# Moving the switch from 8-tile to 16-tile chunks in an edge-sorting message-passing kernel

## The chip, the core and the metric

The kernel runs on one core of a Trainium2 chip. A core has five engines with a queue each: TensorE (PE; PEld is its weight loads), VectorE (DVE), ScalarE (ACT), GpSimd (POOL) and SyncE (SP). Indirect DMAs are issued from POOL, plain loads and stores from SP. The metric is the time of one execution on the device in microseconds (us); less is better. The kernel before was run three times, 11277.25, 11285.53 and 11288.28 us, median 11285.53.

## What is computed

One layer of message passing over a graph with 12,500 nodes of 64 features and 800,000 edges with 16 attributes; every edge has a source and a destination drawn at random.

```python
m_in = jnp.concatenate([x[src], x[dst], e_attr], axis=-1)
msg = _silu(m_in @ w_msg)
agg = _segment_sum(msg, dst, N)
return _silu(jnp.concatenate([x, agg], axis=-1) @ w_upd)
```

## The kernel before

The product with `w_msg` is split: node tables hold `x @ w_msg` for the source part (`A_d`, in memory) and for the destination part (`BW`, on chip). What is left for an edge is a row of `A_d` fetched by its source, a row of `BW` picked by its destination, and the attributes' product. To make the destination part local, the edges are first sorted into 128 buckets of 98 nodes, in memory (`st`), and then worked off in tiles of 128 edges of one bucket. Both halves run together, in one loop of *periods*.

**Sorting.** The edges lie in 6,250 tiles of 128. A *step* takes 8 tiles (`M`). It builds a one-hot of each edge's bucket (`onehot`, L397 and L398, ScalarE), running counts of the buckets over the tiles (`sums` or `halves`, L414 to L425, VectorE and ScalarE), ranks by matmul (`count`, L434 to L440, TensorE, then the reduce L445 on VectorE), spreads each edge's 17-number record to the slot of its rank (`expand`, L455 to L459, VectorE; tile `X`), and sums the tiles by matmul into a block `pl` with a row for each bucket (`move`, L476 and L478, TensorE). ScalarE copies the block (L483, L485) and POOL writes it to the buckets' ends in `st` by one indirect DMA, the *scatter* (L503). The pointers move on by the counts (`place`, L498 and L499).

A block gathers a *chunk*. The first `N8` chunks are one step long (8 tiles, turn 3 in the code), the later ones two steps (16 tiles, turns 0 and 1). `LIM[k]` is the number of slots that the first k+1 tiles of a chunk may fill in a bucket: 10 to 24 for the first eight, 27 to 36 for the second eight. A record has 17 numbers, so the second half's matmuls are 461 to 614 columns wide; what passes 512 goes to a second matmul (L478) into a free part of the PSUM bank of the batch's sums (`ag`). A chunk of 8 multiplies its tiles in falling order of width, a chunk of 16 in rising order.

**Groups and batches.** As soon as whole units of sorted tiles are known to lie in the store, a *group* of them is formed: a prefix sum over the buckets by matmul (L598), a list of tiles (L602 to L604), loads of the tiles from `st` (SP, L586). A group is cut into *batches*, one in a period: POOL gathers rows of `A_d` by source (`gather`, L666, one indirect DMA for each tile), VectorE builds one-hots of the destination (L676), TensorE transposes them (L685), multiplies by `BW` (L694) and, after the sum and the silu (L698, L699), sums the messages by destination (`reduce`, L715, into `ag`), and VectorE adds these sums to `ACC` (L727).

The groups grow. First come 64 tiles in batches of 8, then 640 tiles in groups of 24 with batches of 6 (two tiles to a unit), which are formed *quickly* (L598 right behind the ranks), then groups of 64 with batches of 8 (four tiles to a unit). When a group may be formed is decided while the program is built, by drawing sixteen random histories of the buckets (`Draws`) and waiting until all of them hold enough tiles. A chunk's tiles enter these histories when the chunk ends.

**The order in a period** is written out in `period`: each engine runs its part of the step and of the batches in this order, and each engine's queue keeps it.

```python
if q: q.gather(0, BT // 2)
if s: s.scatter()
if q: q.gather(BT // 2, BT)
```

So a scatter stands between the two halves of a batch's gathers. On TensorE a period holds the ranks of one step, the prefix sum if a quick group is formed, the transposes and sums of the batches, the placing matmuls of the step before, and the batch's product. On VectorE it holds the batch's one-hots, the group's lists, the rank reduce, the batch's sum and the adding to `ACC`, the running counts and the expansion.

After the last step (781) the loop goes on with batches alone until all sorted tiles are used (the *tail*), and the node update closes the kernel.

Of the kernel before, what the change touches and what calls it, by code (L numbers as in the profile page):

```python
# [21 lines left out]
MAGIC = 12582912.0  # L22
M = 8
C = 16
N8 = 140
LIM = [10, 13, 15, 17, 20, 21, 23, 24, 27, 28, 29, 30, 32, 34, 35, 36]
S = LIM[-1]
S8 = LIM[M - 1]
# [21 lines left out]
def mpnn_kernel(tc, x, e_attr, src, dst, w_msg, w_upd, out):  # L50
# [4 lines left out]
    assert E % P == 0 and NB <= NBK and NT >= C  # L55
    K8 = min(N8, NT // (2 * M))
    NCH = K8 + (NT - K8 * M + C - 1) // C
# [1143 lines left out]
```

## Time and profile before

| | |
|---|---|
| median of three runs | 11285.53 us |
| profiled execution | 11177.2 us |
| its span, first to last instruction | 11175.3 us |
| mean granted TensorE clock | 0.881 |
| gathers / scatters in it | 6322 / 460 grouped on one line, 461 in all |
| sort steps | 782 |

The profile is of one execution. It gives, for each engine, the time in which instructions ran; for groups of instructions of a line, their number, busy time and mean; for idle time, what ended it; and all of this for any window of the span. A row of the windows view is: the window, its length, then busy time and instructions of PE, PEld, DVE, ACT and POOL, the granted clock, the DMA share and GB/s. With a line chosen it has the busy time of that line's instructions alone. Matmuls in single precision appear as two records each.

### The profile page before, as it was taken

The page shows a single profiled execution, that of the slowest core. Times are in us where ns is not written, and L with a number is a line of the kernel's source. Part 1 is how long each engine was busy: PE and PEld are TensorE (multiplying, and loading weights), DVE is VectorE, ACT ScalarE, POOL GpSimd, SP SyncE. Part 2 cuts the span into 40 slices and gives each one's busy share as a digit, 9 for nine tenths or more (in the row PEclk, how much of TensorE's full clock was granted, in tenths as well). Part 3 has the DMA queues.
Part 4 walks back from the last instruction along what each step waited for, and adds up shares of the span by engine and source line. Part 5 has one row for each costly group of instructions (what it writes and reads, how often), then busy time and mean ns, then how long its engine had stood idle before and what let it go on. Part 6 is the DMA issues. An engine that isn't in the chain of part 4 may idle for free. (4 is left out here: it accounts for less than half of the span.)

```text
span 11175.3 us, 161538 instructions
## 1 busy us (share of the span) xinstructions
PE 9256.5 (83%) x51526; PEld 6296.5 (56%) x51526; DVE 7890.1 (71%) x17695; ACT 4917.0 (44%) x12471; POOL 6460.2 (58%) x6801
## 2 busy tenths in 40 slices
PE   7788888888888888888888888888888888888566
PEld 5566655555555555555555555555555555555455
DVE  7777777777677777777777777777777777777232
ACT  6455544444444444444444444444444444444111
POOL 2566655555555555555556555555555555555555
PEclk9999989989898988899999898899998988999655
DMA  3122211111111111211111111111111111111222
GB/s 96 44 51 50 51 45 42 44 40 44 39 43 40 44 39 41 45 41 42 42 41 44 42 40 43 40 40 42 43 41 43 41 43 40 43 42 39 41 39 45
DMA packets 667987, 490.31 MB, mean 44 GB/s; under 512 B 497911, under 2 KB 534967, under 8 KB 667127
## 3 DMA queue, kind: packets, MB, share of 16 engines
q0 software_dynamic: 237264, 338.54, 13.8%
q1 hardware_dynamic: 429543, 141.28, 6.0%
q8 instruction: 413, 6.77, 0.3%
q14 instruction: 447, 3.66, 0.1%
q10 hardware_dynamic: 320, 0.07, 0.0%
HBM read 330.05 MB, written 141.12 MB: 42 GB/s over the span
## 5 line engine op out<-in xcount | busy, mean ns | idle before, releaser
L666 POOL DMA_INDIRECT g<-A_d,sidx x6322 | 5993.1, 948 | 3438.0 <-issue 1686.2
L476 PE MATMUL pl<-X,hf 128*128 128x512 f32 (+10 forms) x12512 | 5005.5, 536 | 303.8 <-issue 255.1
L476 PEld LDWEIGHTS pl<-X,hf 128*128 128x128 f32 x12512 | 2358.1, 203 | 1669.7 <-issue 1145.5
L459 DVE TENSOR_TENSOR X<-cb,rec 128x442 f32<-128x442 f32 (+7 forms) x3128 | 2953.7, 1007 | 27.0
L397 ACT ACTIVATE hf<-iof,shi 128x128 f32<-128x128 f32 x6256 | 1908.5, 391 | 985.4 <-remote 569.6
L688 ACT ACTIVATE qt<-tq 114x1024 f32<-114x1024 f32 (+1 forms) x818 | 808.1, 988 | 2392.6 <-remote 1574.5
L727 DVE TENSOR_TENSOR ACC<-ag,ACC 64x98 f32 x1986 | 509.8, 257 | 1538.4 <-remote 1173.7
L445 DVE TENSOR_REDUCE rank<-z 128x8 f32<-128x1024 f32 x782 | 954.3, 1220 | 690.9 <-remote 387.1
L416 DVE TENSOR_TENSOR G<-G,hf 128x128 bf16<-128x128 bf16 x4173 | 1221.1, 293 | 144.9 <-ACT hf L398 4.0
L694 PEld LDWEIGHTS pre<-w,qt 114*128 114x128 f32 x10368 | 1243.2, 193 | 127.4 <-issue 117.8
L694 PE MATMUL pre<-w,qt 114*128 114x64 f32 x10368 | 1246.6, 274 | 24.9 <-issue 15.1
L478 PEld LDWEIGHTS ag<-X,hf 128*128 128x128 f32 x2568 | 549.4, 220 | 1161.5 <-issue 678.3
L483 ACT ACTIVATE blk<-pl 128x512 f32<-128x512 f32 (+1 forms) x461 | 263.2, 571 | 2133.1 <-PE pl L476 1674.8
L503 POOL DMA_INDIRECT st<-blk,ptrs x460 | 460.4, 1001 | 1183.2 <-ACT blk L485 910.8
L685 PE MATMUL tq<-ident,q 128*114 128x128 f32 x6322 | 981.7, 301 | 178.6 <-issue 125.4
L715 PE MATMUL ag<-q,g 128*64 128x98 f32 x12644 | 892.4, 276 | 278.1 <-issue 224.9
L685 PEld LDWEIGHTS tq<-ident,q 128*114 128x114 f32 x6322 | 844.5, 151 | 376.8 <-issue 191.2
L715 PEld LDWEIGHTS ag<-q,g 128*64 128x64 f32 x12644 | 683.7, 152 | 474.3 <-issue 405.0
L398 ACT ACTIVATE hf<-hf,ones 128x1024 f32<-128x1024 f32 x782 | 899.4, 1150 | 25.4
L676 DVE TENSOR_TENSOR q<-cb,lo 128x784 f32<-128x784 f32 (+1 forms) x818 | 768.6, 940 | 81.3 <-PE cb L598 32.3
L478 PE MATMUL ag<-X,hf 128*128 128x34 f32 (+3 forms) x2568 | 501.2, 280 | 360.2 <-DVE ACC L727 347.3
L434 PE MATMUL z<-hf,w 128*128 128x512 bf16 x1564 | 646.5, 413 | 7.8 <-ACT hf L398 5.0
(144 smaller groups left out, 5561.9 us busy)
## 6 DMA issues: line engine op xcount, KB each, us to landing
g<-A_d,sidx POOLq DMA_INDIRECT x6322
ea<-in_e_attr SPq DMA_DIRECT2D x260, 192.0 KB
rt<-st SPq DMA_DIRECT2D x1296, 34.0 KB
rt<-st SPq DMA_DIRECT2D x498, 8.5 KB
st<-blk,ptrs POOLq DMA_INDIRECT x460
nodes<-in_x SPq DMA_DIRECT2D x62, 98.0 KB
ACC<-rt SPq DMA_DIRECT2D x11, 544.0 KB
rt<-st SPq DMA_DIRECT2D x320, 17.0 KB
```

Source lines behind the costliest of these rows:

```text
L397: nc.scalar.activation(c.hf[:, k, :], iof, AF.Square, bias=c.hi[:, k:k + 1])
L398: nc.scalar.activation(c.hf, c.hf, AF.Relu, bias=ones, scale=-1.0)
L416: nc.vector.tensor_tensor(out=at(k), in0=c.hf[:, k - 2, :] if c.pos[k - 1] == 1 else at(k - 1), in1=c.hf[:, k - 1, :], op=OP.add)
L445: nc.vector.tensor_reduce(out=c.rank, in_=c.z, axis=AX.X, op=OP.max)
L459: nc.vector.tensor_tensor(out=c.x[:, k:k + 2, 2:2 + n * R].rearrange("p k (s c) -> p k s c", c=R), in0=hit[:, k:k + 2, 0:n, None].to_broad ...
L476: nc.tensor.matmul(pl[:, 0:min(w, 512)], c.hf[:, k, :], c.x[:, k, 0:min(w, 512)], start=n == first, stop=n == last, skip_group_check=True)
L478: nc.tensor.matmul(pl2[:, 0:w - 512], c.hf[:, k, :], c.x[:, k, 512:w], start=n == WIDE, stop=n == last, skip_group_check=True)
L666: j = nc.gpsimd.indirect_dma_start(out=t.g[:, i, :], out_offset=None, in_=A_d, in_offset=bass.IndirectOffsetOnAxis(ap=t.grp.sidx[:, k:k + ...
L685: nc.tensor.transpose(t.tq[0:KQ, j * P:(j + 1) * P], t.q[:, j, :], ident)
L688: nc.scalar.activation(t.qt[:, 0:w], t.tq[0:KQ, 0:w], AF.Copy)
L694: nc.tensor.matmul(t.pre[:, i * D:(i + 1) * D], t.qt[:, i * P:(i + 1) * P], w, start=True, stop=True)
L715: o = nc.tensor.matmul(t.ag[t.half(v), v // 2 * BK:(v // 2 + 1) * BK], t.g[:, i, :], t.q[:, i, 0:BK], start=(k == 0), stop=(k == u - 1))
```

## The change

One constant:

```diff
-N8 = 140
+N8 = 36
```

Steps 36 to 139 thus belong to 52 chunks of 16 tiles and no longer to 104 chunks of 8. There are 409 chunks and not 461. The capacity of a bucket in `st` follows from the same numbers and is smaller (2,692,352 rows in all against 2,774,272). The groups' sizes and the batches do not depend on `N8`; when they are formed does, through the histories.

What moves, as the program's order has it (buffer numbers are part of the names; `x6` means six in a row). First POOL, in steps of the stretch with batches of 6. Before, a scatter in each step:

```order
L666 DMA g_185<-A_d,sidx 128x64 x4
L503 DMA st<-blk,ptrs 2774272x17
L666 DMA g_185<-A_d,sidx 128x64 x2
L666 DMA g_186<-A_d,sidx 128x64 x4
L503 DMA st<-blk,ptrs 2774272x17
L666 DMA g_186<-A_d,sidx 128x64 x2
```

and with the change one in two steps:

```order
L666 DMA g_185<-A_d,sidx 128x64 x4
L503 DMA st<-blk,ptrs 2692352x17
L666 DMA g_185<-A_d,sidx 128x64 x2
L666 DMA g_186<-A_d,sidx 128x64 x6
L666 DMA g_187<-A_d,sidx 128x64 x4
L503 DMA st<-blk,ptrs 2692352x17
```

The gathers are the same, six to a step. Second, TensorE in a step that ends a chunk, from the batch's sums (L715) over the placing matmuls to the load of the product's registers. Before, in any step of the stretch:

```order
L715 MATMUL ag<-q,g_187 64x98 x6
L476 MATMUL pl<-X_184,hf 128x410
L476 MATMUL pl<-X_184,hf 128x393
L476 MATMUL pl<-X_184,hf 128x359
L476 MATMUL pl<-X_184,hf 128x342
L476 MATMUL pl<-X_184,hf 128x291
L476 MATMUL pl<-X_184,hf 128x257
L476 MATMUL pl<-X_184,hf 128x223
L476 MATMUL pl<-X_184,hf 128x172
L508 TENSOR_LOAD rb
```

and with the change in every second step (the other steps have the same eight as before, in rising order):

```order
L715 MATMUL ag<-q,g_187 64x98 x6
L476 MATMUL pl<-X_184,hf 128x461
L476 MATMUL pl<-X_184,hf 128x478
L476 MATMUL pl<-X_184,hf 128x495
L476 MATMUL pl<-X_184,hf 128x512 x2
L478 MATMUL ag<-X_184,hf 128x34
L476 MATMUL pl<-X_184,hf 128x512
L478 MATMUL ag<-X_184,hf 128x68
L476 MATMUL pl<-X_184,hf 128x512
L478 MATMUL ag<-X_184,hf 128x85
L476 MATMUL pl<-X_184,hf 128x512
L478 MATMUL ag<-X_184,hf 128x102
```

The four L478 write into `ag`, which the L715 ahead of them has just filled and which VectorE reads at L727. Third, VectorE where a quick group is formed, from the end of one step's expansion to the first numbers of the group (`wl`), which the prefix sum L598 on TensorE reads. Before:

```order
L459 TENSOR_TENSOR X_184<-cb,rec 128x2x357
L459 TENSOR_TENSOR X_184<-cb,rec 128x2x408
L498 SCALAR_TENSOR_TENSOR LOST<-blk 128x1
L499 SCALAR_TENSOR_TENSOR ptrs<-blk,LOST,ptrs 128x1
L676 TENSOR_TENSOR q<-cb,lo 128x6x98
L562 SCALAR_TENSOR_TENSOR wl<-ptrs,ub_147 128x1
L563 TENSOR_SCALAR wl<-wl 128x1
```

and with the change:

```order
L459 TENSOR_TENSOR X_184<-cb,rec 128x2x476
L459 TENSOR_TENSOR X_184<-cb,rec 128x2x510
L459 TENSOR_TENSOR X_184<-cb,rec 128x2x578
L459 TENSOR_TENSOR X_184<-cb,rec 128x2x612
L676 TENSOR_TENSOR q<-cb,lo 128x6x98
L562 SCALAR_TENSOR_TENSOR wl<-ptrs,ub_147 128x1
L563 TENSOR_SCALAR wl<-wl 128x1
```

The group's numbers stand behind the wide expansion there, and no pointer update stands between, since no chunk ended in that step. Last, POOL near step 520, where the order with the change has a scatter between two whole batches:

```order
L666 DMA g_187<-A_d,sidx 128x64 x4
L666 DMA g_188<-A_d,sidx 128x64 x8
L503 DMA st<-blk,ptrs 2692352x17
L666 DMA g_185<-A_d,sidx 128x64 x8
L666 DMA g_186<-A_d,sidx 128x64 x4
```

The step of this scatter has no batch of its own. Before, the same gathers run on with one batch in each step from step 37 to the end of the steps:

```order
L666 DMA g_187<-A_d,sidx 128x64 x4
L666 DMA g_188<-A_d,sidx 128x64 x8
L666 DMA g_185<-A_d,sidx 128x64 x4
L503 DMA st<-blk,ptrs 2774272x17
L666 DMA g_185<-A_d,sidx 128x64 x4
```

## The prediction

> **What bounds the kernel now.** I read the page first: its busy times and its row of slices.
>
> ```profile
> span 11175.3 us, 161538 instructions
> PE 9256.5 (83%) x51526; PEld 6296.5 (56%) x51526; DVE 7890.1 (71%) x17695; ACT 4917.0 (44%) x12471; POOL 6460.2 (58%) x6801
> PE   7788888888888888888888888888888888888566
> DVE  7777777777677777777777777777777777777232
> POOL 2566655555555555555556555555555555555555
> PEclk9999989989898988899999898899998988999655
> ```
>
> There are three stretches. TensorE is busy eight tenths of nearly every slice, VectorE seven, and in the last three slices VectorE falls away: there only gathered batches are left. The change touches steps 36 to 139, which lie in slices 2 to 6, so the share over the whole span says little. I cut two windows by the starts of sort steps: steps 48 to 131 (chunks of 8 tiles, batches of 6 gathers) and steps 199 to 758 (chunks of 16, batches of 8). The columns are length, then busy time of PE, PEld, DVE, ACT and POOL, then granted clock, DMA share and GB/s. The second pair of rows are the same windows for the rank reduce (L445), which runs once in a step.
>
> ```profile
> 491.66:1398.42 906.76, 768.61 (x4454) 562.13 (x4454) 709.08 (x1876) 488.29 (x1205) 562.02 (x586) 0.91 0.22 51
> 2287.15:10017.30 7730.15, 6577.30 (x36410) 4351.94 (x36409) 5685.80 (x12286) 3449.87 (x8869) 4524.74 (x4761) 0.90 0.19 42
> ...
> 491.66:1398.42 906.76, 102.26 (x84) 0.91 0.22 51
> 2287.15:10017.30 7730.15, 683.75 (x560) 0.90 0.19 42
> ```
>
> 84 steps take 906.76 us, 10.79 each, or 43.18 for four. 560 later steps take 13.80 each. TensorE is busy 85% of both windows, VectorE 78% and 74%, POOL 62% and 59%. So TensorE ends last, with gaps. What opens the gaps is in the waits of the two windows (total us, times, longest):
>
> ```profile
> PE cb L598 <- DVE wl L563: 55.1, 14, 4.0
> PE cb L598 <- DVE wl L566: 19.2, 4, 5.0
> ...
> PE cb L598 <- DVE X L459: 389.6, 68, 6.2
> PE ag L478 <- DVE ACC L727: 301.9, 109, 3.6
> ```
>
> In the first window TensorE stops for VectorE at the prefix sum of a new group (L598), 18 times for about 4 us. In the second it stops there for 5.7 us at a time, because the wide expansion (L459) stands ahead of it on VectorE, and also at L478, the matmul that only a chunk of 16 has, until VectorE has added the batch's sums out of the same bank (L727).
>
> **The change part by part.** Steps 36 to 139 stay 104 steps with the same gathers beside them: the order shows the same six gathers a step. They become 52 chunks of 16. A group of 24 tiles is still formed every four steps, so I count in fours: 26 of them. The nearest rows are one such four of each kind, one row a step:
>
> ```profile
> 747.73:762.56 14.83, 10.48 (x61) 7.60 (x60) 12.67 (x39) 6.77 (x18) 10.06 (x11) 0.88 0.16 35
> 762.56:774.68 12.12, 9.75 (x55) 7.07 (x52) 8.99 (x25) 5.39 (x14) 6.03 (x7) 0.86 0.25 49
> 774.68:782.75 8.07, 8.07 (x53) 6.12 (x53) 6.01 (x14) 5.58 (x16) 5.48 (x6) 1.00 0.33 80
> 782.75:791.29 8.54, 8.34 (x53) 6.13 (x53) 5.80 (x14) 5.34 (x15) 5.30 (x6) 1.00 0.18 45
> 2506.50:2521.62 15.12, 9.24 (x64) 7.16 (x64) 10.47 (x22) 8.69 (x24) 10.70 (x12) 0.88 0.19 44
> 2521.62:2535.56 13.94, 13.94 (x75) 8.81 (x75) 10.84 (x31) 3.61 (x9) 5.73 (x6) 0.88 0.08 14
> 2535.56:2544.20 8.64, 8.64 (x64) 6.69 (x61) 4.23 (x12) 6.30 (x18) 5.62 (x6) 1.00 0.38 90
> 2544.20:2561.07 16.87, 13.26 (x70) 7.58 (x70) 14.00 (x26) 5.96 (x16) 10.32 (x12) 1.00 0.32 67
> ```
>
> The upper four add to 43.56 us, the lower to 54.57. VectorE works 33.5 us in the upper and 39.5 in the lower, TensorE 36.6 and 45.1. In each four the first step holds the stop for the group.
>
> *Added on TensorE.* The second half of a chunk multiplies by records of 27 to 36 slots instead of 10 to 24, and past 512 columns it needs four more small matmuls into the bank of the batch's sums. The placing matmuls (L476, then L478) in these two fours:
>
> ```profile
> 747.73:791.29 43.56, 19.22 (x64) 12.69 (x64) 0.92 0.22 49
> 2506.50:2561.07 54.57, 24.87 (x64) 11.13 (x64) 0.94 0.23 51
> ...
> 2506.50:2561.07 54.57, 2.81 (x16) 2.95 (x16) 0.94 0.23 51
> ```
>
> 19.22 becomes 27.68 us: 8.5 us more in four steps, nearly all of it on the engine that is busy 85%. Of the ten rank matmuls in two steps (L434 to L440) eight stay; that is inside the lower rows too.
>
> *Added on VectorE.* The expansion grows with the slots and the running counts of two steps become fourteen single adds (L416) where four double and two single ones stood (L424, L425). The lower four hold all of this: 6 us more. It lies beside TensorE's work except at L598 and L478, where TensorE stands behind it. Queued behind those two are the batch's transposes and the next chunk's matmuls; for these wait the scatter and the next group.
>
> *Removed.* 52 scatters on POOL, 52 copies of the block by ScalarE (L483) and 52 pointer updates. POOL, with its issue time, has room (rival 3), so I cost them at nothing. What hides them is TensorE's chain, which the row of waits shows last; without that cover they are the 82 us of rival 3.
>
> *From fours of 16 to this stretch.* For a steady price I take twelve fours with one group in them, first and last of the twelve and the sum:
>
> ```profile
> 2287.15:2342.27 55.12, 46.41 (x266) 31.13 (x266) 39.65 (x90) 24.97 (x65) 32.27 (x35) 0.91 0.23 50
> ...
> 3503.05:3557.70 54.65, 45.64 (x266) 30.09 (x266) 39.48 (x90) 24.57 (x64) 32.29 (x35) 0.94 0.23 50
> sum 661.38, PE 553.96 PEld 368.50 DVE 481.27 ACT 297.66 POOL 388.12; mean PE 46.16 PEld 30.71 DVE 40.11 ACT 24.80 POOL 32.34
> ```
>
> 661.38 / 12 = 55.12 us. These gather eight tiles a step; the changed stretch gathers six, so eight tiles in four steps come off. The trace before has no stretch of 16-tile chunks with six, so the price of a gathered tile is bounded from both sides. Low: the two steps above that TensorE fills entirely, 8.64 us with eight tiles and 8.07 with six, both with the same eight narrow placing matmuls:
>
> ```profile
> 774.68:782.75 8.07, 4.39 (x16) 2.94 (x16) 1.00 0.33 80
> 2535.56:2544.20 8.64, 4.39 (x16) 2.85 (x16) 1.00 0.38 90
> ```
>
> That is 0.57 us for two tiles, 0.285 a tile. High: steps before the first gather, which carry no tile, against the steps with six:
>
> ```profile
> 86.60:165.00 78.40, 14.68 (x12) 1.00 0.39 121
> ```
>
> 78.40 / 12 = 6.53 us; (10.79 - 6.53) / 6 = 0.71 us a tile, the group's stops included. A four has both full steps and stops, so neither row is nearer: I take 0.5, half way. Eight tiles are then 4.0 us (2.3 to 5.7), and a four takes 51.1 us (49.4 to 52.8). Against 43.18 that is 7.9 us more (6.3 to 9.6), and 26 fours give **206 us** (163 to 251).
>
> *Moved: the supply.* Sorted tiles become known one step later on average. In the order no batch is missing from step 37 to the end before; after the change one is, at step 520, where the scatter follows eight gathers at once. The batch runs in the tail instead, where only gathers are left:
>
> ```profile
> 10314.00:11138.00 824.00, 480.85 (x510) 0.59 0.26 42
> ```
>
> 824 / 510 x 8 = 12.9 us for a batch there. The step that goes without gains 8 x 0.285 to 8 x 0.71 = 2.3 to 5.7 us, so the net is 7 to 11; I take **8**. Ahead of that step and behind it the order is of the same kind as before.
>
> The sum is 206 + 8 = 214 us. It is made against the profiled execution (11177.2 us, span 11175.3); the median of the runs, 11285.53, lies 108 above it, and I add the sum to that: **11500 us**, 1.9% slower.
>
> **The rivals.** *1. Fewer tiles save nothing.* VectorE, not TensorE, sets the four: its work hardly falls with six tiles a batch, since groups with two tiles to a unit add three sums (L727) where the others add two. For it: the stops at L598 and L478 are both waits for VectorE. Against: TensorE fills several whole steps. The four stays at 55.12: 11.94 x 26 + 8 = 318 us, 11604 us.
>
> *2. The gaps take the work.* TensorE's gaps in the first window are 906.76 - 768.61 = 138.2 us, 6.6 in a four. If the 8.5 us fall into them, 1.9 is left: 1.9 x 26 + 8 = 57 us, 11343. Against: the gaps are waits for VectorE, which gets 6 us of its own ahead of the same stops.
>
> *3. POOL decides, and the kernel gets faster.* Its place is the POOL queue, where the scatter stands between the two halves of a batch's gathers and holds back the second half. Its price, from the first window:
>
> ```profile
> 491.66:1398.42 906.76, 83.95 (x84) 0.91 0.22 51
> ...
> L666 POOL DMA_INDIRECT g<-A_d,sidx x6322 | 5993.1, 948 | 3438.0 <-issue 1686.2
> ...
> POOL g L666 <- issue: 130.2, 417, 3.4
> POOL st L503 <- ACT blk L483: 24.5, 17, 1.8
> POOL st L503 <- issue: 23.5, 58, 1.1
> ```
>
> A scatter is 83.95 / 84 = 1.00 us plus (24.5 + 23.5) / 84 = 0.57 of waiting; 52 of them are 82 us, and the time would be 11204. It decides from the point where POOL has no gap left. It has: 562 busy + 154 of issue are 79% of the window, and the lower fours run POOL 32 us in 55. [...]
>
> *4. The change doesn't do what it says.* It calls step 36 the last wait for sorted tiles, and the order has one more. That is the 8 us above and no more, unless the real counts at step 520 hold the group back longer, which nothing before shows.
>
> **How the numbers follow.** Forecast 0.70 (fours of 49.4 to 52.8 us, 11457 to 11545), rival 1 and worse 0.15, rival 2 and what lies between it and the forecast 0.09, rival 3 0.05, nothing at all 0.01. The range reaches to rival 1 above and somewhat past half way to rival 2 below: 11390 to 11610. A measurement of this kernel tells about 0.2%, 23 us, from no change. Faster by more: 0.05 (rival 3). Within: 0.02. Slower by more: 0.93.
>
> **What would show it.** Right: the 84 steps that took 906.76 us take about 1073, steps alternating between some 8 us and some 16; matmuls of L478 from step 37 on; TensorE stopping at L598 for longer than 4 us and at L478 for VectorE; POOL's gathers unchanged at 948 ns; one batch more after the last sort step, in a tail some 13 us longer. Wrong: steps of even length near 11 us (rival 2), a stretch of about 1160 us with VectorE without gaps (rival 1), or gathers closing up behind missing scatters (rival 3).

## The result, and the profile after

| | before | changed |
|---|---|---|
| median on the same chip, us | 11281.39 (4 runs) | 11382.87 (4 runs) |
| ratio, 95% interval | 1 | 1.0093 [1.0071, 1.0114] |
| profiled execution, us (span) | 11177.2 (11175.3) | 11380.2 (11378.4) |

The changed kernel is slower by 101 us (80 to 129 by the interval), where 214 were forecast. The direction is right, the size is not half. The profiled executions differ by 203 us, which looks like the forecast and isn't: the profiled execution of before was 104 us faster than the median of its runs, and the changed one's 3 us. So the time has to be found stretch by stretch.

The page of the changed kernel, busy times and slices:

```profile
span 11378.4 us, 161109 instructions
...
PE 9370.2 (82%) x51077; PEld 6365.6 (56%) x51838; DVE 8059.7 (71%) x17959; ACT 4879.9 (43%) x12435; POOL 6399.4 (56%) x6749
...
PE   7888888888888888888888887888888888888556
DVE  7888887777777777777777776777777777777222
...
PEclk9899998888898888888998888889889888899655
```

Against the page before, TensorE and VectorE carry 114 and 170 us more, POOL 61 less. VectorE's slices 2 to 6 have gone from seven tenths to eight.

The window of steps 48 to 131, cut at the rank reduces (L445), columns as in the prediction. Before:

```profile
494.28:1403.44 909.16, 767.28 (x4442) 560.98 (x4438) 712.72 (x1882) 489.04 (x1206) 563.81 (x588) 0.91 0.22 50
```

The same window of the changed kernel:

```profile
507.87:1515.26 1007.39, 881.13 (x4620) 590.22 (x4702) 853.51 (x2140) 458.75 (x1153) 527.88 (x546) 0.93 0.19 41
```

84 steps take 98 us more: a four goes from 43.3 us to 48.0, not to 51.1. VectorE gets 6.7 us a four more (141 / 21), TensorE 5.4 (114 / 21). Four steps of the changed kernel one by one (steps 56 to 59):

```profile
608.24:623.45 15.21, 14.97 (x70) 9.74 (x72) 10.38 (x38) 7.54 (x22) 5.57 (x6) 0.81 0.08 21
623.45:635.07 11.62, 11.56 (x72) 8.17 (x72) 10.41 (x22) 6.93 (x18) 7.02 (x8) 1.00 0.35 61
635.07:643.96 8.89, 8.13 (x40) 4.89 (x39) 8.55 (x22) 4.16 (x12) 5.32 (x6) 1.00 0.20 53
643.96:656.14 12.18, 7.33 (x45) 5.31 (x44) 10.95 (x26) 6.59 (x16) 7.16 (x8) 0.95 0.16 37
```

The step with the formed group is followed by one at a clock of 0.81, in which TensorE is busy nearly from end to end and yet takes 15.2 us; in the last step, at whose end the next stop for a group lies, VectorE is busy for 10.95 of 12.18 us and TensorE for 7.33. What the engines wait for in steps 48 to 131 (total us, times, longest):

```profile
ACT blk L483 <- PE pl L476: 195.7, 24, 9.2
POOL g L666 <- PE ag L715: 170.6, 55, 6.7
...
POOL st L503 <- ACT blk L485: 119.3, 34, 5.0
...
PE cb L598 <- DVE wl L566: 95.6, 21, 5.7
...
ACT qt L688 <- remote: 43.8, 20, 2.4
...
PE ag L478 <- DVE ACC L727: 12.5, 17, 1.7
```

TensorE's stop for VectorE at the prefix sum is there 21 times, once in each four, 4.6 us long. Before it was there 20 times in the same steps, 82.3 us in all, so of the 98 us it has 13. The forecast's second stop, at L478, hardly shows: 12.5 us in 21 fours.

Outside the stretch, windows of steps 515 to 539, where the batch is missing, and of the tail. Before:

```profile
6644.95:6996.53 351.58, 297.19 (x1635) 196.43 (x1635) 255.12 (x549) 152.70 (x393) 204.33 (x216) 0.89 0.20 44
...
10314.00:11175.00 861.00, 515.61 (x3178) 447.47 (x3176) 244.34 (x646) 154.88 (x299) 486.82 (x516) 0.59 0.25 41
```

The same two of the changed kernel:

```profile
6801.12:7167.69 366.57, 296.32 (x1598) 196.10 (x1620) 253.66 (x555) 153.33 (x395) 196.48 (x208) 0.86 0.18 41
...
10501.90:11378.00 876.10, 524.51 (x3218) 457.23 (x3216) 233.46 (x599) 158.56 (x320) 493.24 (x524) 0.60 0.25 41
```

The tail is 15 us longer. The 25 steps around the missing batch are 15 us longer too, not shorter. Of the kernels in the sections below, four on another chip of this sort run the program of before or the changed one in these 25 steps: two as before take 345.8 and 349.1 us there, two as changed 367.4 and 371.0. So the step without a batch costs some 15 to 25 us here. Steps 150 to 514, the same program in both, differ by 38 us in these two executions (5024.3 and 5062.1). On that other chip they take 5049.4 to 5056.2 us, with and without the change, so it is the one execution of before that was fast. The stretch of 104 steps takes 1135.3 us before and 1251.3 after, +116. If the execution of before is scaled to its median (11281.39 / 11177.2), the stretch costs 105 us, the 25 steps 12 and the tail 7, 124 in all, which lies in the interval of the medians; this is an estimate.

### The profile page after: what moved, and what is told of

Read it like the earlier page. It is cut to its first block, busy times and chain, and to the rows that moved or that the text cites. A ratio compares the mean times of both kernels' runs of the same rounds, so it can differ in the third digit from the quotient of the medians.

```text
span 11378.4 us, 161109 instructions
## 1 busy us (share of the span) xinstructions
PE 9370.2 (82%) x51077; PEld 6365.6 (56%) x51838; DVE 8059.7 (71%) x17959; ACT 4879.9 (43%) x12435; POOL 6399.4 (56%) x6749
## 5 line engine op out<-in xcount | busy, mean ns | idle before, releaser
L476 PE MATMUL pl<-X,hf 128*128 128x512 f32 (+9 forms) x12512 | 5261.5, 557 | 288.9 <-issue 236.5
L476 PEld LDWEIGHTS pl<-X,hf 128*128 128x128 f32 x12512 | 2370.4, 205 | 1641.7 <-issue 1143.5
L459 DVE TENSOR_TENSOR X<-cb,rec 128x442 f32<-128x442 f32 (+7 forms) x3128 | 3051.5, 1038 | 28.2 <-DVE cb L456 1.2
L688 ACT ACTIVATE qt<-tq 114x1024 f32<-114x1024 f32 (+1 forms) x818 | 806.8, 986 | 2762.4 <-remote 1975.2
L727 DVE TENSOR_TENSOR ACC<-ag,ACC 64x98 f32 x1938 | 497.6, 257 | 1703.4 <-remote 1368.8
L416 DVE TENSOR_TENSOR G<-G,hf 128x128 bf16<-128x128 bf16 x4849 | 1417.7, 292 | 165.9 <-ACT hf L398 3.6
L478 PEld LDWEIGHTS ag<-X,hf 128*128 128x128 f32 x2984 | 669.7, 231 | 1508.3 <-issue 821.0
L445 DVE TENSOR_REDUCE rank<-z 128x8 f32<-128x1024 f32 x782 | 953.8, 1220 | 513.4 <-remote 302.7
L694 PE MATMUL pre<-w,qt 114*128 114x64 f32 x10496 | 1274.3, 275 | 39.4 <-issue 22.6
L503 POOL DMA_INDIRECT st<-blk,ptrs x408 | 407.3, 998 | 1368.4 <-ACT blk L485 1096.9
L478 PE MATMUL ag<-X,hf 128*128 128x34 f32 (+3 forms) x2984 | 604.5, 289 | 523.0 <-DVE ACC L727 512.9
L715 PE MATMUL ag<-q,g 128*64 128x98 f32 x12644 | 826.5, 268 | 131.9 <-issue 127.8
L676 DVE TENSOR_TENSOR q<-cb,lo 128x784 f32<-128x784 f32 (+1 forms) x818 | 768.7, 940 | 79.3 <-PE cb L598 48.1
L715 PEld LDWEIGHTS ag<-q,g 128*64 128x64 f32 x12644 | 641.6, 146 | 278.4 <-issue 265.4
L436 PE MATMUL z<-G,onesb 128*128 128x512 bf16 (+1 forms) x1491 | 579.3, 389 | 74.5 <-issue 38.4
```

The source lines that it names most:

```text
L416: nc.vector.tensor_tensor(out=at(k), in0=c.hf[:, k - 2, :] if c.pos[k - 1] == 1 else at(k - 1), in1=c.hf[:, k - 1, :], op=OP.add)
L445: nc.vector.tensor_reduce(out=c.rank, in_=c.z, axis=AX.X, op=OP.max)
L459: nc.vector.tensor_tensor(out=c.x[:, k:k + 2, 2:2 + n * R].rearrange("p k (s c) -> p k s c", c=R), in0=hit[:, k:k + 2, 0:n, None].to_broad ...
L476: nc.tensor.matmul(pl[:, 0:min(w, 512)], c.hf[:, k, :], c.x[:, k, 0:min(w, 512)], start=n == first, stop=n == last, skip_group_check=True)
L478: nc.tensor.matmul(pl2[:, 0:w - 512], c.hf[:, k, :], c.x[:, k, 512:w], start=n == WIDE, stop=n == last, skip_group_check=True)
L688: nc.scalar.activation(t.qt[:, 0:w], t.tq[0:KQ, 0:w], AF.Copy)
```

## The experiments

The runs fell on further chips, of two kinds. Where before takes 11150 to 11290 us, as above, I say the slower kind; where it takes 9012, the faster. Kernels are compared with before on the same chip; steps are compared across chips only within a kind.

### The same pair again, and the change over more or fewer steps (faster kind)

```diff
-N8 = 140
+N8 = 36
```

and 88 and 390 at the same place: chunks of 8 up to that step.

> The kernel before, once more, so that both profiles come from one chip. If the two profiles differ by 203 us only because they were taken at different places, this profile's span is near 11275 and its steps 150 to 515 take as long as those of the changed kernel (within 10 us, where the first two profiles lie 38 us apart). If the changed kernel is truly slower there, they lie 38 apart again.

> The changed kernel beside it. Theory (a fixed price for each of the 104 steps): steps 36 to 139 take 110 to 120 us longer than in the kernel before, the missing batch at step 520 and the longer tail 15 to 25, all else nothing; sum 125 to 145 us in the profile. Rival (something later gives back): the stretch costs 115, but the rest is 10 to 30 us shorter than before, and the times differ by 100.

> The switch at step 88, half way between the two: 52 of the 104 steps keep chunks of 8, and the order has no step without a batch. Fixed price: half of what the stretch costs, 52 to 60 us over the kernel before, and nothing for a missing batch. If the cost sat in the missing batch at step 520 or in the tail, and not in the stretch: 0 to 15 us.

> The switch after the last step but two: chunks of 8 nearly throughout. If the price of a 16-tile chunk is its own work (wider matmuls and expansion), the other 640 steps get 1.1 us shorter each or more, 700 us in all or more, about 10570. Rival: with eight gathers and a scatter in each step POOL or the waits of VectorE set the step, as in steps 27 to 31 of the kernel before (12.4 to 13.5 us against 13.8): 250 us or less are gained, or the time rises.

| N8 | median, us | ratio to before (9014.28 us beside these runs), 95% interval |
|---|---|---|
| 140 | 9011.45 | 1.0000 [0.9990, 1.0010] |
| 36 | 9297.08 | 1.0313 [1.0296, 1.0331] |
| 88 | 9156.68 | 1.0155 [1.0138, 1.0171] |
| 390 | 9077.70 | 1.0069 [1.0052, 1.0086] |

The change costs 283 us here, almost three times as much, and half of the steps cost half: 142. In the profiled executions steps 36 to 139 take 921.3 us before and 1192.3 changed, 271 more, the tail 12 more. Steps 150 to 514 take 4040.5 and 4039.6: they do not differ here, as they should not. The window of steps 48 to 131 of before on this chip:

```profile
430.67:1175.15 744.48, 694.05 (x4368) 524.28 (x4452) 702.66 (x1884) 482.90 (x1205) 566.53 (x585) 1.00 0.26 61
```

Of the changed kernel:

```profile
458.29:1428.89 970.60, 870.02 (x4620) 586.15 (x4702) 850.69 (x2139) 460.48 (x1162) 523.39 (x546) 0.94 0.19 43
```

The stop at L598 among the waits of that window, before:

```profile
PE cb L598 <- DVE wl L566: 20.6, 21, 1.9
```

and changed:

```profile
PE cb L598 <- DVE wl L566: 82.9, 21, 4.8
```

VectorE's busy time is that of the slower kind within 1.5%. What differs is before: the 84 steps take 744 us, not 909, TensorE fills 93% of them at full clock and stops at L598 for 1 us in a four. With the change the stop is 4 us and the clock 0.94, much as on the slower kind. So on this chip the change ends a stretch almost without gaps, such as the slower kind does not have there (84% busy at a clock of 0.91): +226 us in 84 steps, of which TensorE's busy time is 176.

The slower kind had waits to give up. There "remote" in the views is a wait that a signal ended and no instruction's end in the profile; at the three lines below, which read what TensorE has written, the signal is TensorE's. The same window of before on the slower kind:

```profile
ACT qt L688 <- remote: 111.8, 43, 3.9
...
DVE rank L445 <- remote: 50.0, 20, 4.0
...
DVE ACC L727 <- remote: 18.5, 11, 2.5
```

Of these 180 us the changed kernel has 47 left (43.8 at L688, 3.1 at L727). So 133 us of waiting went as the work came, and the change is 128 us cheaper there than here (98 against 226). That the one pays for the other is read from the waits and not shown by a run.

Chunks of 8 up to step 389 gain nothing either; steps 200 to 359 take 11.35 us each, against 11.05 with chunks of 16. There ScalarE's copy of the block waits for a scatter to land (waits of steps 200 to 359 of the run with N8 = 390),

```profile
ACT blk L483 <- DMA st<-blk,ptrs: 687.1, 146, 5.7
```

and TensorE, in turn, for the copy:

```profile
PE pl L476 <- ACT blk L483: 124.1, 93, 2.3
```

ScalarE's wait is 4.3 us a step. It looks like another limit than the one studied here, met by chunks of 8 where batches have eight tiles; no run took it out.

### The prefix sum behind the batch's sums (slower kind)

```diff
-            for g in quick:
-                g.middle()
-                g.k = 1
             if t:
                 t.transpose(0)
...
             if r:
                 r.reduce()
+            for g in quick:
+                g.middle()
+                g.k = 1
```

Beside it stands a version in which groups of four-tile units do this too (`free`): their prefix sum, which stood at the end of the step, is held and issued in the next step at the new place, and the group's second part follows behind the expansion.

```diff
-            quick = [g for g in forms if g.quick and g.k == 0]
+            quick = [g for g in forms if g.k == 0 and (g.quick or g.held)]
...
             for g in forms:
+                if g.k == 0 and early:
+                    g.held = True
+                    continue
                 g.middle()
```

> The changed kernel with one thing moved: for groups of two-tile units the prefix sum (L598) stands on TensorE behind the batch's transposes and sums instead of ahead of them. Theory: the price of the change is TensorE's added work at full clock (about 5.7 us a four, from busy times with the half-clock windows taken out) plus the stop at L598 of 4 us and the half-clock window behind it (1.4 to 1.8 us a step). With useful work ahead of the stop it falls under 2 us, the half-clock windows of steps 48 to 131 fall under 0.5 us a step, and a four goes from 46 to 48 us to 41 to 43.5: 65 to 150 us less in all than the changed kernel. Rival (VectorE's work sets the four, the stop is only where it shows): the four stays within 1 us and the whole time within 30 us of the changed kernel.

> The kernel before with the same move of L598. Theory: on a chip where its stop is short (1 us, clock 1.00 in steps 48 to 131) 0 to 30 us less than before; where the stop is 4 us and the clock 0.91, 80 to 150 us less. The difference between the changed kernel and this one, both with the move, is then TensorE's work of 26 fours, 150 to 200 us, on either kind of chip. Rival: no difference to before, and the price of the change stays what it was without the move.

> The changed kernel with the move of L598, and for groups of four-tile units too: their prefix sum, which stood at the end of a step and waited for the wide expansion (L459) that reads the same PSUM bank, stands in the next step behind the batch's sums. Theory: the stop of 2.5 to 6 us in every eight steps and the half-clock windows behind it go, in the whole stretch from step 140 to 760: clock from 0.97 to 1.00, and beyond the gain of the run with two-tile units alone 200 to 430 us less where the stop was 2.5 us, more where it was 6. Rival (VectorE sets the steps of 16 tiles): less than 100 us beyond that run, and the wait shows up at another line.

> The kernel before with both moves. Theory: 200 to 460 us less than before, and the fastest of the four; the changed kernel with both moves is 150 to 200 us above it. Rival: within 100 us of before.

| | changed kernel | kernel before |
|---|---|---|
| as it is (other chips of the kind) | 1.0093 [1.0071, 1.0114]; 1.0082 [1.0051, 1.0112] | 1 |
| L598 moved for two-tile units | 1.0053 [1.0035, 1.0070] | 0.9971 [0.9954, 0.9988] |
| moved for all | 0.9976 [0.9959, 0.9993] | 0.9909 [0.9877, 0.9941] |

The window of steps 48 to 131 of the changed kernel with the first move:

```profile
505.31:1445.50 940.19, 873.92 (x4721) 574.77 (x4720) 851.64 (x2140) 458.52 (x1154) 524.32 (x546) 0.96 0.20 44
```

and its stop at L598 among the waits:

```profile
PE cb L598 <- DVE wl L566: 12.9, 7, 3.3
```

The stop falls from 95.6 us to 12.9, the clock rises from 0.93 to 0.96, and the 84 steps take 67 us less than on the first chip: a four of 44.8 us, where I expected 41 to 43.5 and the rival 47 to 49. The half-clock time fell from 1.75 us a step to 0.83, not to 0.5. In the whole time the gain is 0.3 to 0.4%, 32 to 45 us, less than the 65 expected. In the kernel before the move took the stop from 82.3 us to 54.0 only, and it gained 17 us by the medians, not 80 to 150. The changed kernel stays 84 us above it, not 150 or more, where 101 and 107 were measured without the move: on the slower kind the stop is a part of the price of the change, and by the whole times most of the price stays without it.

The move for four-tile units gained another 0.6 and 0.8%, which is the rival's result (under 100 us); with both moves the changed kernel stays 75 us above before, where 150 to 200 were expected. TensorE still stands at L598 in the later steps, now with no wait that the profile shows (waits of steps 200 to 359, before with both moves):

```profile
ACT qt L688 <- remote: 363.0, 70, 6.9
...
PE cb L598 <- issue: 82.2, 19, 5.2
```

### TensorE's and VectorE's price, one at a time

Twice the product matmuls of the batches of six tiles, and twice their one-hot, each result the same the second time:

```diff
                     for i in range(u * t.grp.u, (u + 1) * t.grp.u):
-                        nc.tensor.matmul(t.pre[:, i * D:(i + 1) * D], t.qt[:, i * P:(i + 1) * P], w, start=True, stop=True)
+                        for _ in range(2 if t.grp.u == 2 else 1):
+                            nc.tensor.matmul(t.pre[:, i * D:(i + 1) * D], t.qt[:, i * P:(i + 1) * P], w, start=True, stop=True)
```

```diff
-                nc.vector.tensor_tensor(out=t.q[:, 0:n, 0:BK], in0=ioB[:, None, :].to_broadcast([P, n, BK]), in1=t.grp.lo[:, i0:i0 + n, None].to_broadcast([P, n, BK]), op=OP.is_equal)
+                for _ in range(2 if t.grp.u == 2 else 1):
+                    nc.vector.tensor_tensor(out=t.q[:, 0:n, 0:BK], in0=ioB[:, None, :].to_broadcast([P, n, BK]), in1=t.grp.lo[:, i0:i0 + n, None].to_broadcast([P, n, BK]), op=OP.is_equal)
```

> The changed kernel again, as the base of the runs beside it. If the kernel before takes about 11150 to 11300 us on this chip, 80 to 110 us more than before; if it takes about 9010, 270 to 300 us more.

> The kernel before with the twelve product matmuls (L694) of each of the 106 batches of six tiles issued twice, the second time with the same result: 1.36 us of TensorE work a step at 0.113 us each, 144 us in all, in the steps that the change touches. TensorE's chain sets the steps: +110 to +150 us on a chip of either kind. Rival, the gaps take the work: under +50 us.

> The kernel before with the one-hot of the same batches (L676, 0.76 us) issued twice, with the same result: 81 us of VectorE work. VectorE's work lies beside TensorE's except ahead of the stop for a new group: where TensorE fills 93% of the steps (before at 9010 us) 0 to +30 us; where VectorE waits for late signals of TensorE and TensorE then for VectorE (before at 11150 to 11300) +40 to +80 us, since both stand in one loop.

> The changed kernel with the same second issue of the product matmuls, 144 us of TensorE work. TensorE sets the steps of the stretch: +110 to +150 us on the changed kernel. VectorE sets them (88% busy there): under +60 us.

> The changed kernel with the one-hot of the 106 batches of six tiles issued twice, 81 us of VectorE work. If VectorE's work sets the price of the change: +50 to +80 us on the changed kernel, against +20 on the kernel before; if VectorE lies beside TensorE: under +25 us.

| kernel | kind | ratio to before, 95% interval |
|---|---|---|
| changed | slower | 1.0082 [1.0051, 1.0112] |
| before, TensorE's work doubled | slower | 1.0028 [1.0018, 1.0037] |
| before, VectorE's work doubled | slower | 1.0018 [1.0002, 1.0033] |
| changed, TensorE's work doubled | slower | 1.0115 [1.0087, 1.0142] |
| changed, VectorE's work doubled | faster | 1.0407 [1.0390, 1.0424] |

The windows of steps 48 to 131. Before with TensorE's work doubled:

```profile
501.89:1446.09 944.20, 833.37 (x5386) 645.93 (x5471) 708.30 (x1883) 498.80 (x1204) 563.23 (x588) 0.99 0.21 49
```

Before with VectorE's doubled:

```profile
498.88:1447.20 948.32, 765.83 (x4350) 565.27 (x4432) 774.79 (x1966) 490.86 (x1204) 565.05 (x588) 0.90 0.21 48
```

The changed kernel with TensorE's doubled:

```profile
514.98:1543.75 1028.77, 959.45 (x5628) 682.72 (x5710) 857.63 (x2139) 470.44 (x1162) 527.55 (x546) 0.98 0.18 41
```

and, on the faster kind, with VectorE's doubled:

```profile
465.16:1501.93 1036.77, 876.39 (x4620) 588.26 (x4702) 914.37 (x2223) 464.55 (x1162) 523.19 (x546) 0.92 0.18 40
```

On the slower kind 114 us of TensorE work in these 84 steps (84 x 12 matmuls of 0.113 us) cost 35 before the change (944.2 - 909.2) and 21 after it (1028.8 - 1007.4; the changed kernel took 1007.4 us on this chip as on the first). The rows say where the rest went before the change. TensorE's busy time rose by 66 us only, with the clock from 0.91 to 0.99, so the faster clock gave back 48 of the 114; another 31 fell into idle time. I had expected +110 to +150 us in all; +0.28%, 31 us, is the rival's result, and so are the 32 us on the changed kernel.

62 us of VectorE work cost 39 by the same account, 0.63 us for one against 0.31. But both are taken against the one execution of before on the first chip, which was 104 us faster than its median. Scaled to the median it gives 0.49 and 0.23. The whole times, all on one chip, give 20 us (2 to 37) for 81 of VectorE's, where I had expected 40 to 80, and 31 (20 to 42) for 144 of TensorE's: 0.25 and 0.22. So neither engine's work is charged one to one there; that VectorE's is the dearer is not shown.

On the faster kind VectorE's price in the changed steps is one to one: 64 us more busy, 66 us longer (1036.8 - 970.6), and in all +81 us for 81 issued (9377.61 - 9297.08, the same chip). So in the changed steps VectorE lies in the loop that sets the time there. That TensorE set these steps before the change is read from its 93% at full clock; neither doubling was run on the kernel before in these steps on this kind.

### The price of a tile, and of TensorE's work in the later steps (faster kind)

Batches of eight tiles and groups of 32 for the two-tile units, a group still in every four steps; and the products of the four-tile units doubled in the kernel before.

```diff
-FIRST = [(1, 48, BT, (1, 0, 1, 0)), (2, 24, 6, (3, 3, 2, 2))]
+FIRST = [(1, 48, BT, (1, 0, 1, 0)), (2, 32, 8, (3, 3, 2, 2))]
```

> The changed kernel with batches of eight tiles and groups of 32 in place of six and 24 for the two-tile units, so that a group is still formed every four steps. Sorted tiles then run short at times; steps 56 to 96 have a batch each. Read there, a four takes 47.97 us plus the price of eight tiles. If the forecast's half microsecond a tile holds: about 52 us, and the rest of the 55.1 is the kind of group. If tiles explain all of the difference: about 55 us (0.9 a tile). If VectorE and TensorE's signals, not tiles, set the four: within 1.5 us of 48.

> The changed kernel with eight tiles a step and groups of 32, again; steps 56 to 96 are read. On the slower kind a four took 47.8 us there with six tiles: near 50 us if a tile costs 0.27 us as on the faster kind (the later fours are then dearer by 5 us for their kind of group), near 52 at the forecast's 0.5, near 55 if tiles explain the whole difference. On the faster kind 48.2 us again.

> The kernel before with the product matmuls of all batches of four-tile units issued twice: 16 x 0.113 = 1.8 us of TensorE work a step, about 1050 us over the steps 145 to 780 at full clock and some in the tail. If TensorE's work sets these steps, +900 to +1200 us and steps of 15.4 us or more. If, as in the steps of eight tiles, most of it is taken back because TensorE then runs at full clock: +200 to +500 us and the granted clock near 0.97 there.

The window of steps 56 to 95 of the changed kernel with six tiles:

```profile
554.86:1015.20 460.34, 414.35 (x2200) 279.67 (x2240) 404.43 (x1017) 219.12 (x553) 248.96 (x260) 0.93 0.19 43
```

and with eight:

```profile
552.74:1034.57 481.83, 439.16 (x2620) 304.25 (x2661) 431.93 (x1037) 234.52 (x554) 325.95 (x342) 0.96 0.23 49
```

Ten fours take 21.5 us more: 2.15 a four, 0.27 a tile. A second run, on another chip of the kind, gave 48.04 us a four against 48.18. On this kind my half microsecond was nearly twice too much, and the lower bound (0.285) was the right row. On this kind a four of the later steps, eight tiles with four-tile units, takes 44.2 us (11.05 a step), 4 less than eight tiles with two-tile units. So the later fours differ from those of the stretch in more than the tiles.

The window of steps 200 to 359 of before on this kind:

```profile
1910.93:3679.57 1768.64, 1701.24 (x10242) 1191.17 (x10401) 1606.47 (x3509) 979.24 (x2533) 1300.16 (x1362) 0.97 0.22 52
```

and with the doubled products:

```profile
1986.27:3959.44 1973.17, 1950.67 (x12810) 1451.06 (x12970) 1610.15 (x3509) 1002.13 (x2534) 1306.58 (x1361) 1.00 0.20 47
```

1.28 us a step for 1.8 issued, and 1.0916 [1.0898, 1.0934] or 826 us in all, between the two expectations: TensorE sets most of these steps' time. Of the 0.53 us a step that it didn't cost, 0.25 came back through the clock (TensorE's busy time rose by 1.56 us a step) and 0.28 went into idle time. On the slower kind this was not run.

### Both moves on the faster kind

> The changed kernel with both moves of the prefix sum, again. On a chip where before takes 9010 us: VectorE's work counts one to one in the changed steps, and with TensorE's stop of 4 us out of its loop the 84 steps go from 970 us to 860 to 920 (VectorE's own 851 is the floor); in the later steps the stop of 2.5 us and the half-clock window behind it go, 200 to 430 us over the whole stretch. On a chip of the slower kind: within 0.3% of what it was there (0.9976 of before).

> The kernel before with both moves, again. On a chip where before takes 9010 us: the 84 steps within 15 us of their 744, 200 to 430 us less over the later steps, and the fastest version there; the changed kernel with both moves 140 to 220 us above it instead of 283. On the slower kind: 0.991 of before again.

8778.71 us and 0.9741 [0.9725, 0.9757] for before with both moves, 8992.48 us and 0.9979 [0.9969, 0.9988] for the changed kernel with them. The windows of steps 48 to 131 and 200 to 359 of the changed kernel with the moves:

```profile
454.69:1374.06 919.37, 848.27 (x4638) 567.98 (x4720) 849.63 (x2140) 461.23 (x1163) 522.81 (x548) 0.97 0.20 45
...
2098.79:3802.73 1703.94, 1662.66 (x10240) 1160.80 (x10400) 1603.39 (x3509) 979.50 (x2533) 1291.00 (x1356) 1.00 0.23 54
```

and of before with them:

```profile
427.02:1171.82 744.80, 697.83 (x4382) 531.44 (x4464) 702.79 (x1884) 484.00 (x1206) 566.53 (x586) 0.98 0.26 62
...
1877.45:3584.07 1706.62, 1663.96 (x10240) 1160.80 (x10400) 1604.57 (x3508) 979.99 (x2534) 1293.08 (x1358) 1.00 0.23 54
```

With the moves the stop at L598 in the changed steps falls from 82.9 us to 53.7 and the clock rises from 0.94 to 0.97; the steps take 51 us less (970.6 to 919.4), before's none, and the price of the change falls from 283 to 214 us. So a quarter of it went with the two moves. What is left in 84 steps, 175 us, is near the 147 us that VectorE is busy more, and as near the 150 us of TensorE; no run here tells which of the two sets it. Before with both moves beats both kernels on either kind: by 0.9% and by 2.6%.

## Why the prediction was wrong

- **The stretch.** 206 us were forecast for 104 steps (163 to 251); 116 were measured between the profiled executions, 105 by the scaled estimate above. The step that failed is the term **"From fours of 16 to this stretch"**: 55.12 less eight tiles at 0.5 us, 51.1 us. Measured are 48.0, below the lower end of 49.4. The two halves of that step fail in opposite ways. The tiles were taken at half way between 0.285 and 0.71; the faster kind shows 0.27, which would have made the four 53 us and the forecast worse. Within the forecast's own bounds no price of a tile leads from 55.12 to 48.0 us; it would take 0.89. So the starting row doesn't seem to belong: the later fours are no fours of the stretch with two more tiles a step. Steps 200 to 359 of before, on the slower kind, carry waits that the changed stretch hardly has:

```profile
ACT qt L688 <- remote: 313.2, 57, 7.5
DVE ACC L727 <- remote: 252.0, 95, 3.6
...
PE cb L598 <- DVE X L459: 112.0, 19, 6.0
```

The remote waits at these two lines are 14.1 us in a four there ((313.2 + 252.0) / 40) and 2.2 in the changed stretch. They are waits for TensorE's signals, and the prediction did not ask whether the row that it took as nearest had the same waits as the place it was carried to. On the faster kind no such waits show (the same steps have no remote row of 7 us or more), and the same step would have erred the other way: less than 44.2 us, what a later four takes, in place of the 46.2 that the stretch took. The price of a tile on the slower kind was not measured, so a dearer tile there stays possible.
- **"So TensorE ends last, with gaps."** Not on this kind of chip. 114 us of added TensorE work cost 35 (27 against the scaled execution): part of TensorE's 85% was time at half clock, of which there was less with the added work (granted clock 0.91 and 0.99), and 31 us of the work fell into its gaps. The stops for VectorE, named in the same part, are there, but moving the prefix sum was worth 17 us before the change and 32 to 45 after it. With the prices of the doubled runs in this window (0.31 and 0.63) the change's own work would cost 37 us for TensorE (120 us at full clock, the half-clock time taken off both busy times) and 89 for VectorE (141), 126 us in 84 steps; with those of the whole times (0.22 and 0.25) 62; 98 were measured. These are estimates, and the forecast of 167 for these steps lies outside them.
- **Work added.** TensorE's placing matmuls were forecast at 8.5 us a four and VectorE's work at 6; the rows give 8.5 (L476 and L478 together 583.6 us against 404.2 in 21 fours) and 6.7. The work was priced well, its effect was not.
- **Removed.** 52 scatters were costed at nothing. POOL's gathers stayed at 947 ns, and with POOL busy 36 us less in the window the steps got longer. Rival 3 did not come true. The DMA share of the window is 0.22 before and 0.19 after.
- **The missing batch.** The tail was forecast 12.9 us longer and is 15.1; on the faster kind it is 11.8 longer, while on the slower kind's other chip the changed kernel's tail (880.4) lies between those of the two versions of before (875.3 and 884.7). The gain in the step without a batch (2.3 to 5.7 us) did not show: these 25 steps took 15 to 25 us more on the slower kind and 2.3 on the faster (277.6 and 279.9). Why they do is open.
- **The rivals.** Rival 2, the gaps take the work, was given 0.09 at 57 us; on the slower kind the truth lies between it and the forecast, 44 us from the one and 113 from the other. Rival 1, VectorE sets the four, is what the doubled one-hot showed on the faster kind, where the change costs 283 us; its price of 318 came from the wrong row and lies near by luck.
- **The signs.** 84 steps of 1073 us: 1007. Steps alternating between some 8 and 16: 15.2, 11.6, 8.9, 12.2. Stops at L598 above 4 us: yes, 4.6. Waits at L478: no. The range missed by 7 us, because its lower end was put at a little over half way to rival 2 and that rival's share was set too low.

What stays open: why TensorE's signals come late on the slower kind, and whether its later fours are dearer for that alone.

## What to carry to other kernels

A price taken from another stretch is to be trusted only if that stretch waits for the same things: compare the rows of waits before the durations. Busy time at a granted clock below 1 was no bound here (at 0.91, 114 us of added TensorE work cost 35); adding a little work to the engine and seeing what it costs says in one run what its busy share doesn't. A small matmul that waits for another engine, here the prefix sum, belongs behind the work that is ready already, not ahead of it: the moves took between 0.3% (the first alone, kernel before, slower kind) and 3.3% (both, changed kernel, faster kind) off the time.

## What the runs showed of the hardware

The kernel before takes a median of 9012 to 9014 us on two chips and of 11147 to 11281 on the others, with nearly the same durations on VectorE and POOL (in steps 48 to 131 VectorE is busy for 712.7 us on the slower kind and 702.7 on the faster, and a gather takes 953 and 960 ns). In steps 200 to 359 of before on the slower kind the copy of the transposes (L688) starts a median of 1.38 us after the last transpose's modelled end, in 63 of 160 cases more than 3 us after, and its remote waits are 313.2 us, 57 of them, the longest 7.5. On the faster kind the waits of the same steps, down to rows of 7.0 us, have no remote one at any line.

In the profile of before on the slower kind the granted clock is 1.00 or 0.50, in stretches of 3.41 us or a multiple of it (all of the 710 records but one). Cut into pieces of 3.41 us, steps 200 to 759 have 1493 pieces at full clock in which TensorE idled for under 1.05 us in all, and none of these was followed by a piece at half clock; of the 220 with 1.75 us or more, 217 were, and of the 109 in between, 30. In steps 200 to 359 of the same profile each of the 20 stops at L598, 3.9 to 6.0 us long, has time at half clock in it or within 3.41 us behind it. On the faster kind these steps of before have 51.7 us of such stops, the longest 3.1, at a clock of 0.97, and with both moves 27.9 us, the longest 2.7, at 1.00.

The stop at L598 in groups of four-tile units was no wait for its operand. At the 20 stops of steps 200 to 359 of before, on the slower kind, VectorE had written `wl` 10.5 to 14.1 us before L598 ran, and at 19 of them TensorE waited for the end of the expansion (L459; 112.0 us, the longest 6.0), whose source `hit` is another slice of the PSUM tile `cb` that holds the prefix sum. On the faster kind the wait for L459 is there 20 times (51.7 us). Issued in the next step L598 waits 1.4 us there in place of 2.6, and the steps fall from 11.05 to 10.67 us. The wait that is left (steps 200 to 359 of before with both moves, faster kind) is for VectorE's one-hot L676, which reads a third slice of `cb`:

```profile
PE cb L598 <- DVE q L676: 27.9, 20, 2.7
```

That the shared tile is the reason is read from the program and the releasers of both waits; no run took the prefix sum out of the tile.
